# A hand-ordered software pipeline on every engine, exp(L) left in PSUM, and dummy matmuls first, in a fused gated-linear-attention and max-out kernel

## The chip, the cores and the metric

The kernel runs on one core of a Trainium2 chip. The metric is the device time of one execution in microseconds; lower is better. Here a run counts as slow when it is over 1.5% above the fastest run of the same kernel. A profile is one execution and covers its span, which is about 1.8 us shorter than the reported time. Below, "unit" is one step of the kernel's main loop: one chunk of 128 positions for two of the four batches. There are 12 units.

## The reference

```python
state = alpha[:, :, t, :, None] * state + einsum('bhd,bhe->bhde', k[:, :, t], v[:, :, t])   # for t in range(768)
y[:, :, t] = einsum('bhd,bhde->bhe', q[:, :, t], state)
x = y.transpose(0, 2, 1, 3).reshape(B * S, H * D)        # 3072 x 384
out = maximum(x @ w1, x @ w2) @ w_out                     # d_ff = 1024
```

B = 4, H = 8, S = 768, D = 48, all fp32. The kernel works in chunks: L is the running sum of log alpha in a chunk, q is scaled by exp(L), k by exp(-L), and the state is carried from chunk to chunk. The maximum is rewritten as relu(x(w1 - w2)) + x w2, so that x w2 w_out can be added by one small product, `w2o` = w2 w_out, made once.

## The kernel before

Each unit runs `gla(u)`: `lg` = Ln(alpha); the sums `cs` on TensorE; `Em` = exp(-L), `Ep` = exp(L) on ScalarE; `kn` = k x `Em` on GpSimd; `qn` = q x `Ep` on VectorE; transposes `tp`, copied to `qk`; the state products `kv`, added into `tm`; scores `pp`, masked into `pt`; outputs `ya`, cast to `xn`, transposed to `xp`, copied to `xt`. Then `moe(u-1)`: four hidden blocks `hp` with a relu into `gT`, and two output blocks `op`, copied to `outs`. A scheduler of the programming layer reorders what the program lists.

```python
nc.scalar.activation(out=Em, in_=csv[bb], func=ACTF.Exp, scale=-1.0)
nc.scalar.activation(out=Ep, in_=csv[bb], func=ACTF.Exp)                 # Ep in SBUF
nc.gpsimd.tensor_mul(out=kn[:, :, 0:D], in0=t["kf"][:, bb], in1=Em)
nc.vector.tensor_mul(out=qn[:, :, 0:D], in0=t["qf"][:, bb], in1=Ep)
# ... (cut)
for u in range(NU):
    if u + 3 < NU:
        load(u + 3)
    gla(u)
    if u == 0:
        weights()          # w2h -> transposes wt -> w2T; wo16; wq -> w2o; w12 = w1f - w2f
    if u - LAG >= 0:
        moe(u - LAG)       # LAG = 1
```

## Time and profile before

| | before |
|---|---|
| time, median (3 runs) | 189.61 us |
| span of the profile | 187.8 us |
| PE / DVE / ACT / POOL busy | 80 / 58 / 41 / 29% |
| period of a unit, undisturbed (125 to 139 us) | 13.15 us |
| first hidden matmul of unit 0 | 26.66 us |

The start: the timeline of the kernel before (start, duration, engine and line, instruction, and in brackets how long the engine idled before it and what ended that).

```profile
17.85 2.94 ACT L131 CAST w2h<-w2f 128x1024 f16<-128x1024 f32 x3
23.41 3.41 PE L142 MATMUL wq<-wo,w2T 128*128 128x384 f16 x20 [0.87 <-DVE wo L138]
27.39 1.36 PE L278 MATMUL hp<-xt,w 128*128 128x256 f16 x11 [0.46 <-ACT w2o L146]
30.29 0.50 PE L173 MATMUL cs<-lg,mc 64*128 64x384 f16 x4
```

The weights are cast and multiplied between 17.85 and 27 us, while the loads of unit 1 are still under way; its `cs` follows at 30.29.

### The profile page before, as it was taken

How to read it: one execution, taken by the hardware profiler on the slowest of the kernel's cores; microseconds unless marked ns; L12 is line 12 of the kernel's file. 1: busy time of each engine (PE TensorE's matmuls, PEld its weight loads, DVE VectorE, ACT ScalarE, POOL GpSimd, SP SyncE). 2: the span in 40 equal slices, each digit the busy share in tenths (PEclk: the TensorE clock that was granted, in tenths of full speed). 3: DMA queues.
4: the chain of work that ended last, by engine and by line, in shares of the span. 5: the costliest groups of instructions: out<-in, count | busy, mean ns of one | idle time of the engine just before them, and what ended most of it. 6: DMA issues, size and time to landing. Idle time of an engine off the chain costs nothing.

```text
span 187.8 us, 3984 instructions
## 1 busy us (share of the span) xinstructions
PE 149.7 (80%) x1632; PEld 98.8 (53%) x1632; DVE 109.4 (58%) x189; ACT 76.7 (41%) x163; POOL 53.7 (29%) x70
## 2 busy tenths in 40 slices
PE   0276799959997886976997896996996978969991
PEld 0063556627656545545554655654555545646660
DVE  4076773955939839647525846928919739358110
ACT  2503438237155361560236236346245364363331
POOL 5230302407208026035006407209018036061000
PEclk9999999966999999996579999999999999999999
DMA  4999999997998985969912994956957720020012
GB/s 106 188 338 377 378 187 186 169 246 152 194 182 206 201 210 105 162 162 153 155 31 87 199 168 130 204 103 165 172 141 152 133 84 5 0 84 3 10 74 84
DMA packets 92098, 28.56 MB, mean 152 GB/s; under 512 B 87216, under 2 KB 91312, under 8 KB 92080
## 3 DMA queue, kind: packets, MB, share of 16 engines
q1 hardware_dynamic: 88816, 23.60, 67.8%
q10 hardware_dynamic: 3264, 4.72, 6.8%
q8 instruction: 12, 0.20, 0.5%
q14 instruction: 6, 0.05, 0.1%
HBM read 23.59 MB, written 4.72 MB: 151 GB/s over the span
## 4 chain that ended last, share of the span: by engine, by line
PE 32%; issue 28%; DVE 17%; POOL 8%; ACT 7%; DMA 4%; ACTq 1%; SPq 1%; POOLq 0%; DVEq 0%
PE op L292 10%; DVE qn L190 6%; DVE pt L239 4%; PE op L290 4%; POOL kn L189 4%; DMA qf<-in_q_dram 4%; PE hp L278 3%; PE tp L194 3%; PE ya L256 3%; PE pp L237 2%; DVE tm L224 2%; DVE qk L196 2%; PE xp L265 2%; PE wq L142 2%; ACT outs L295 2%
## 5 line engine op out<-in xcount | busy, mean ns | idle before, releaser
L189 POOL TENSOR_TENSOR kn<-kf,Em 128x384 f16<-128x384 f32 x24 | 26.9, 1141 | 105.5 <-ACT Em L187 105.5
L190 DVE TENSOR_TENSOR qn<-qf,Ep 128x384 f16<-128x384 f32 x24 | 26.9, 1158 | 35.6 <-ACT Ep L188 28.9
L278 PE MATMUL hp<-xt,w 128*128 128x256 f16 x288 | 41.3, 284 | 2.0 <-ACT gT L283 1.5
L292 PE MATMUL op<-wo,gT 128*128 128x384 f16 x192 | 39.9, 333 | 0.3 <-DVE gT L285 0.3
L283 ACT ACTIVATE gT<-hp 128x512 f16<-128x512 f32 x36 | 20.8, 625 | 29.2 <-PE hp L278 29.1
L239 DVE TENSOR_TENSOR pt<-pp,u 128x512 f16<-128x512 f32 x48 | 31.2, 686 | 2.5 <-PE pp L237 1.9
L278 PEld LDWEIGHTS <-w 128*128 128x128 f16 x288 | 27.3, 101 | 7.1 <-issue 2.0
L260 ACT CAST xn<-ya 128x384 f16<-128x384 f32 x24 | 11.5, 477 | 31.1 <-PE ya L256 30.3
L295 ACT COPY outs<-op 128x384 f32<-128x384 f32 x24 | 11.5, 479 | 29.8 <-PE op L292 29.8
L292 PEld LDWEIGHTS <-gT 128*128 128x128 f16 x192 | 17.4, 99 | 10.3 <-DVE gT L285 1.5
L194 PE MATMUL tp<-ident,qn 128*128 128x128 f16 x96 | 9.9, 229 | 15.3 <-DVE qn L190 15.3
L290 PE MATMUL op<-w2o,xt 128*128 128x384 f16 x72 | 18.3, 332 | 0.2
L196 DVE COPY qk<-tp 128x1024 f16<-128x1024 f16 x24 | 16.2, 685 | 2.9 <-PE tp L194 2.0
L237 PE MATMUL pp<-qk 48*128 48x128 f16 x192 | 15.6, 232 | 1.3 <-DVE pt L239 0.9
L194 PEld LDWEIGHTS <-qn 128*128 128x128 f16 x96 | 6.1, 101 | 19.8 <-DVE qn L190 19.6
L267 DVE COPY xt<-xp 128x768 f16<-128x768 f16 x12 | 6.7, 557 | 16.1 <-PE xp L265 16.1
L256 PE MATMUL ya<-v,pt 128*128 128x48 f16 x192 | 13.5, 192 | 3.2 <-DVE pt L239 3.0
L187 ACT ACTIVATE Em<-cs 128x384 f32<-128x384 f32 x24 | 11.9, 494 | 8.1 <-PE cs L176 8.1
L256 PEld LDWEIGHTS <-pt 128*128 128x128 f16 x192 | 9.8, 101 | 9.7 <-DVE pt L239 4.7
L285 DVE TENSOR_SCALAR gT<-hp 128x512 f16<-128x512 f32 x12 | 8.2, 684 | 10.1 <-PE hp L278 10.0
L237 PEld LDWEIGHTS <-qk 48*128 48x128 f16 x192 | 9.4, 99 | 8.6 <-issue 5.0
L224 DVE TENSOR_TENSOR tm<-kv,sb 64x192 f32<-64x192 f32 x32 | 11.3, 354 | 1.5 <-PE kv L216 1.2
(48 smaller groups left out, 153.2 us busy)
## 6 DMA issues: line engine op xcount, KB each, us to landing
af<-in_alpha_dram SPq DMA_DIRECT2D x24, 192.0 KB, 5.0
kf<-in_k_dram SPq DMA_DIRECT2D x12, 384.0 KB, 5.0
qf<-in_q_dram SPq DMA_DIRECT2D x12, 384.0 KB, 7.0
vf<-in_v_dram SPq DMA_DIRECT2D x12, 384.0 KB, 7.5
out_dram<-outs ACTq DMA_DIRECT2D x12, 384.0 KB, 2.5
w2f<-in_moe_w_dram SPq DMA_DIRECT2D x1, 1536.0 KB, 8.5
wof<-in_moe_w_out_dram SPq DMA_DIRECT2D x1, 1536.0 KB, 10.6
w1f<-in_moe_w_dram SPq DMA_DIRECT2D x1, 1536.0 KB, 14.0
```

The lines of the kernel that those rows point to most:

```text
L189: nc.gpsimd.tensor_mul(out=kn[:, :, 0:D], in0=t["kf"][:, bb], in1=Em)
L190: nc.vector.tensor_mul(out=qn[:, :, 0:D], in0=t["qf"][:, bb], in1=Ep)
L194: nc.tensor.transpose(tp[:, n, j, :], pair(src, j), ident)
L196: nc.vector.tensor_copy(out=qk, in_=tp)
L237: nc.tensor.matmul(pa[a][:, j, :], lhsT=qk[r, 1, j, :], rhs=qk[r, 0, j, :], start=True, stop=True)
L239: nc.vector.tensor_mul(out=pt[:, a], in0=pa[a], in1=u16.unsqueeze(1).to_broadcast([128, HP, C]))
L256: nc.tensor.matmul(o, lhsT=l, rhs=r, start=a not in firsts, stop=(n >= len(mms) - 2))
L278: nc.tensor.matmul(hp[:, n, :], lhsT=w12[:, ds, f * 128 : (f + 1) * 128], rhs=xt[:, ds].rearrange("p n t -> p (n t)"), start=(ds == 0), st ...
L283: nc.scalar.activation(out=gT[:, 2 * f2 : 2 * f2 + 2, :], in_=hp, func=ACTF.Relu)
L290: nc.tensor.matmul(op, lhsT=xt[:, ds, n, :], rhs=w2o[:, ds, :], start=(ds == 0), stop=False)
L292: nc.tensor.matmul(op, lhsT=gT[:, f, n * C : (n + 1) * C], rhs=wo16[:, f, :], start=False, stop=(f == NF - 1))
L295: nc.scalar.copy(out=outs[:, n, :], in_=op)
```

## The change

The intent: TensorE should never wait for a chain of unit u, because between any two steps of that chain stands a piece of the MoE of unit u-1; every engine gets its program in a fixed order. exp(L) overwrites L in PSUM, so that `qn` no longer reads two SBUF operands (1158 ns in the mean in the kernel before). Twelve dummy matmuls on zeros come first, to warm TensorE's clock (the first `cs` group took 0.50 us with them and 0.82 without, E1). The steps are cut out of `gla` and `moe` as small functions (cut here). Smaller changes go with it: `kn` is transposed ahead of `qn`, `wo16` is cast on three engines and not on two, the loads are ordered earlier (unit u+5 at the end of iteration u, not u+3 at its start), and `outs` and `xt` have one buffer fewer each. The core is:

```diff
-            nc.scalar.activation(out=Ep, in_=csv[bb], func=ACTF.Exp)
+            nc.scalar.activation(out=csv[bb], in_=csv[bb], func=ACTF.Exp)
-            nc.vector.tensor_mul(out=qn[:, :, 0:D], in0=t["qf"][:, bb], in1=Ep)
+        nc.vector.tensor_mul(out=X["qn"][bb][:, :, 0:D], in0=X["qf"][:, bb], in1=X["csv"][bb])
+    ctx.enter_context(tc.manual_schedule())
+    warm = new("m", [128, 512], FP32, 2, "warm")
+    for n in range(NWARM):                                   # 12
+        nc.tensor.matmul(warm, lhsT=wz[:, 0:128], rhs=wz, start=True, stop=True)
+    load(1); ln(0); vcast(0); sums(0)                        # shortened to one line
+    for bb in range(2):
+        qmul(0, bb)
+        turn(0, bb)
+    ln(1)
+    vcast(1)
+    # loads of units 2 to 4 (cut)
+    for u in range(NU):
+        nxt = u + 1 < NU
+        kv(u)
+        pairs(u, 0)
+        fill(u, 0)
+        fill(u, 1)
+        if nxt:
+            sums(u + 1)
+        ystate(u)
+        pairs(u, 1)
+        fill(u, 2)
+        fill(u, 3)
+        if nxt:
+            state(u + 1)
+            for bb in range(2):
+                qmul(u + 1, bb)
+        yin(u)
+        fill(u, 4)
+        # turn(u + 1, 0), xturn(u), turn(u + 1, 1), fill(u, 5), ln(u + 2), vcast(u + 2), load(u + 5) (cut)
+    for n in range(6):
+        fill(NU, n)
```

`fill(u, 0..3)` are the hidden blocks and `fill(u, 4..5)` the output blocks of unit u-1; for u = 0 they are the preparation of the weights. `sums` also issues the exps and `kn`.

More of the change, by code (lines that the diff above doesn't have):

```diff
@@ L59 @@
     nc.scalar.preload_act_table_set("natural_log_exp_and_others")
-    loads = {}
+    st = {}
     def load(u):
         c, g = divmod(u, NG)
-        t = {}
+        t = st[u] = {}
         t["af"] = ldp.tile([128, H, 2, D], FP32, tag="af", name="af")
@@ L77, in load @@
             )
-        loads[u] = t
     load(0)
@@ L86 @@
     nc.sync.dma_start(out=w1f, in_=moe_w1.rearrange("(s p) f -> p s f", p=128))
+    NWARM = 12
+    wz = constp.tile([128, 512], FP16)
+    nc.vector.memset(wz, 0.0)
     mc = constp.tile([128, 2, C], FP16)
@@ L127 @@
     w2o = wp.tile([128, ND, DM], FP16)
-    def weights():
-        for ds in range(ND):
-            nc.scalar.copy(out=w2h[:, ds, :], in_=w2f[:, ds, :])
-            wt = psp.tile([128, NF, 128], FP16, tag="m", bufs=2, name="wt")
-            for f in range(NF):
-                nc.tensor.transpose(wt[:, f, :], w2h[:, ds, f * 128 : (f + 1) * 128], ident)
-            nc.vector.tensor_copy(out=w2T[:, :, ds * 128 : (ds + 1) * 128], in_=wt)
-        h2 = NF // 2
-        nc.gpsimd.tensor_copy(out=wo16[:, 0:h2], in_=wof[:, 0:h2])
-        nc.vector.tensor_copy(out=wo16[:, h2:NF], in_=wof[:, h2:NF])
-        for ds in range(ND):
-            wq = psp.tile([128, DM], FP32, tag="m", bufs=2, name="wq")
-            for f in range(NF):
-                nc.tensor.matmul(
-                    wq, lhsT=w2T[:, f, ds * 128 : (ds + 1) * 128], rhs=wo16[:, f, :],
-                    start=(f == 0), stop=(f == NF - 1),
-                )
-            nc.scalar.copy(out=w2o[:, ds, :], in_=wq)
-        for ds in range(ND):
-            nc.vector.tensor_sub(out=w12[:, ds, :], in0=w1f[:, ds, :], in1=w2f[:, ds, :])
@@ L150, with new @@
-    xts = {}
-    carry = {}
     def pair(t, j):
         return t[:, 2 * j : 2 * j + 2, :].rearrange("p h w -> p (h w)")
-    def gla(u):
-        c, g = divmod(u, NG)
-        t = loads.pop(u)
-        last = c == NCH - 1
-        lg = LG[u % NB]
-        nc.scalar.activation(
-            out=lg[:, :, :, 0:D], in_=t["af"].rearrange("p h j d -> p j h d"), func=ACTF.Ln
-        )
-        v16 = gp.tile([128, 2, H, D], FP16, tag="v16", name="v16")
-        nc.gpsimd.tensor_copy(out=v16, in_=t["vf"])
-        cs = [psp.tile([128, 512], FP32, tag="g", bufs=4, name="cs") for _ in range(2)]
-        csv = [x[:, 0 : H * D].rearrange("p (h d) -> p h d", h=H) for x in cs]
+    def new(tag, shape, dtype, bufs, name):
+        return psp.tile(shape, dtype, tag=tag, bufs=bufs, name=name)
@@ new lines, in ln, with vcast, sums @@
+    def ln(u):
+        X = st[u]
+        X["lg"] = LG[u % NB]
+        nc.scalar.activation(
+            out=X["lg"][:, :, :, 0:D], in_=X["af"].rearrange("p h j d -> p j h d"), func=ACTF.Ln
+        )
+    def vcast(u):
+        X = st[u]
+        X["v16"] = gp.tile([128, 2, H, D], FP16, tag="v16", name="v16")
+        nc.gpsimd.tensor_copy(out=X["v16"], in_=X["vf"])
+    def sums(u):
+        X = st[u]
+        c, g = divmod(u, NG)
+        lg = X["lg"]
+        cs = [new("g", [128, 512], FP32, 4, "cs") for _ in range(2)]
+        X["csv"] = csv = [x[:, 0 : H * D].rearrange("p (h d) -> p h d", h=H) for x in cs]
@@ L178, in gla @@
                 )
-        de = gp.tile([128, HP, 2, 2], FP32, tag="de", name="de")
-        qks = []
-        kns = []
+        X["qn"], X["kn"] = [], []
         for bb in range(2):
             qn, kn = QN[(2 * u + bb) % (2 * NB)], KN[(2 * u + bb) % (2 * NB)]
-            kns.append(kn)
-            Ep = gp.tile([128, H, D], FP32, tag="Ep", name="Ep")
+            X["qn"].append(qn)
+            X["kn"].append(kn)
             Em = gp.tile([128, H, D], FP32, tag="Em", name="Em")
             nc.scalar.activation(out=Em, in_=csv[bb], func=ACTF.Exp, scale=-1.0)
-            nc.scalar.activation(out=Ep, in_=csv[bb], func=ACTF.Exp)
-            nc.gpsimd.tensor_mul(out=kn[:, :, 0:D], in0=t["kf"][:, bb], in1=Em)
-            nc.vector.tensor_mul(out=qn[:, :, 0:D], in0=t["qf"][:, bb], in1=Ep)
-            tp = psp.tile([128, 2, HP, C], FP16, tag="g", bufs=4, name="tp")
-            for n, src in ((0, qn), (1, kn)):
-                for j in range(HP):
-                    nc.tensor.transpose(tp[:, n, j, :], pair(src, j), ident)
-            qk = gp.tile([128, 2, HP, C], FP16, tag="qk", name="qk")
-            nc.vector.tensor_copy(out=qk, in_=tp)
-            qks.append(qk)
+            nc.scalar.activation(out=csv[bb], in_=csv[bb], func=ACTF.Exp)
+            nc.gpsimd.tensor_mul(out=kn[:, :, 0:D], in0=X["kf"][:, bb], in1=Em)
@@ L198, in gla @@
+        X["de"] = de = gp.tile([128, HP, 2, 2], FP32, tag="de", name="de")
         nc.scalar.activation(out=de, in_=dps, func=ACTF.Exp)
-        sb = None
         if c:
-            tm, de0 = carry.pop(g)
+            Y = st[u - NG]
             dd = gp.tile([128, 2, HP], FP32, tag="dd", name="dd")
             nc.gpsimd.tensor_mul(
-                out=dd, in0=de0[:, :, :, 0].rearrange("p j b -> p b j"),
+                out=dd, in0=Y["de"][:, :, :, 0].rearrange("p j b -> p b j"),
                 in1=de[:, :, :, 1].rearrange("p j b -> p b j"),
@@ L208, in gla @@
             )
-            sb = gp.tile([128, 2, HP, D], FP16, tag="sb", name="sb")
-            nc.gpsimd.tensor_mul(out=sb, in0=tm, in1=dd.unsqueeze(3).to_broadcast([128, 2, HP, D]))
-        if not last:
-            tm = gp.tile([128, 2, HP, D], FP32, tag="tm", name="tm")
-            for bb in range(2):
-                kv = psp.tile([128, HP, 2 * D], FP32, tag="g", bufs=4, name="kv")
-                for j in range(HP):
-                    nc.tensor.matmul(
-                        kv[:, j, :], lhsT=pair(kns[bb], j), rhs=v16[:, bb, 2 * j : 2 * j + 2, :],
-                        start=True, stop=True,
-                    )
-                for a in range(2):
-                    r = slice(64 * a, 64 * a + 64)
-                    e = slice(D * a, D * a + D)
-                    if c:
-                        nc.vector.tensor_add(out=tm[r, bb], in0=kv[r, :, e], in1=sb[r, bb])
-                    else:
-                        nc.vector.tensor_copy(out=tm[r, bb], in_=kv[r, :, e])
-            carry[g] = (tm, de)
@@ L229, in gla, with state @@
-        pts = []
-        for bb in range(2):
-            qk = qks[bb]
-            pt = gp.tile([128, 2, HP, C], FP16, tag="pt", name="pt")
-            pa = [psp.tile([128, HP, C], FP32, tag="pp", bufs=2, name="pp") for _ in range(2)]
+            X["dd"] = dd
+    def state(u):
+        X = st[u]
+        if u >= NG:
+            X["sb"] = gp.tile([128, 2, HP, D], FP16, tag="sb", name="sb")
+            nc.gpsimd.tensor_mul(
+                out=X["sb"], in0=st[u - NG]["tm"], in1=X["dd"].unsqueeze(3).to_broadcast([128, 2, HP, D])
+            )
@@ new lines, in qmul, with turn @@
+    def qmul(u, bb):
+        X = st[u]
+        nc.vector.tensor_mul(out=X["qn"][bb][:, :, 0:D], in0=X["qf"][:, bb], in1=X["csv"][bb])
+    def turn(u, bb):
+        X = st[u]
+        tp = new("g", [128, 2, HP, C], FP16, 4, "tp")
+        for n, src in ((1, X["kn"][bb]), (0, X["qn"][bb])):
+            for j in range(HP):
+                nc.tensor.transpose(tp[:, n, j, :], pair(src, j), ident)
+        qk = gp.tile([128, 2, HP, C], FP16, tag="qk", name="qk")
+        nc.vector.tensor_copy(out=qk, in_=tp)
+        X["qk", bb] = qk
@@ new lines, in kv @@
+    def kv(u):
+        X = st[u]
+        c, g = divmod(u, NG)
+        if c == NCH - 1:
+            return
+        tm = X["tm"] = gp.tile([128, 2, HP, D], FP32, tag="tm", name="tm")
+        for bb in range(2):
+            kvp = new("g", [128, HP, 2 * D], FP32, 4, "kv")
+            for j in range(HP):
+                nc.tensor.matmul(
+                    kvp[:, j, :], lhsT=pair(X["kn"][bb], j), rhs=X["v16"][:, bb, 2 * j : 2 * j + 2, :],
+                    start=True, stop=True,
+                )
+            for a in range(2):
+                r = slice(64 * a, 64 * a + 64)
+                e = slice(D * a, D * a + D)
+                if c:
+                    nc.vector.tensor_add(out=tm[r, bb], in0=kvp[r, :, e], in1=X["sb"][r, bb])
+                else:
+                    nc.vector.tensor_copy(out=tm[r, bb], in_=kvp[r, :, e])
@@ new lines, in pairs @@
+    def pairs(u, bb):
+        X = st[u]
+        qk = X["qk", bb]
+        pt = X["pt", bb] = gp.tile([128, 2, HP, C], FP16, tag="pt", name="pt")
+        pa = [new("pp", [128, HP, C], FP32, 2, "pp") for _ in range(2)]
+        for j in range(HP):
+            for a in range(2):
+                r = slice(64 * a, 64 * a + D)
+                nc.tensor.matmul(pa[a][:, j, :], lhsT=qk[r, 1, j, :], rhs=qk[r, 0, j, :], start=True, stop=True)
+        for a in range(2):
+            nc.vector.tensor_mul(out=pt[:, a], in0=pa[a], in1=u16.unsqueeze(1).to_broadcast([128, HP, C]))
@@ L234, in gla, with ystate @@
+    def ystate(u):
+        X = st[u]
+        X["ya"] = ya = [new("g", [128, 2, HP, D], FP32, 4, "ya") for _ in range(2)]
+        X["begun"] = begun = set()
+        if u < NG:
+            return
+        for bb in range(2):
             for j in range(HP):
@@ L236, in gla @@
                     r = slice(64 * a, 64 * a + D)
-                    nc.tensor.matmul(pa[a][:, j, :], lhsT=qk[r, 1, j, :], rhs=qk[r, 0, j, :], start=True, stop=True)
-            for a in range(2):
-                nc.vector.tensor_mul(
-                    out=pt[:, a], in0=pa[a], in1=u16.unsqueeze(1).to_broadcast([128, HP, C])
-                )
-            pts.append(pt)
-        ya = [psp.tile([128, 2, HP, D], FP32, tag="g", bufs=4, name="ya") for _ in range(2)]
-        mms = [[], []]
-        for bb in range(2):
-            for j in range(HP):
-                for a in range(2):
-                    if c:
-                        r = slice(64 * a, 64 * a + D)
-                        mms[0].append((ya[a][:, bb, j, :], qks[bb][r, 0, j, :], sb[r, bb, j, :], a))
-                    mms[1].append((ya[a][:, bb, j, :], pts[bb][:, a, j, :], v16[:, bb, 2 * j + a, :], a))
@@ L253, in gla @@
-        mms = mms[0] + mms[1]
-        firsts = set()
-        for n, (o, l, r, a) in enumerate(mms):
-            nc.tensor.matmul(o, lhsT=l, rhs=r, start=a not in firsts, stop=(n >= len(mms) - 2))
-            firsts.add(a)
-        xn = gp.tile([128, 2, HP, 2, D], FP16, tag="xn", name="xn")
+                    nc.tensor.matmul(
+                        ya[a][:, bb, j, :], lhsT=X["qk", bb][r, 0, j, :], rhs=X["sb"][r, bb, j, :],
+                        start=a not in begun, stop=False,
+                    )
@@ new lines, in ystate, with yin @@
+                    begun.add(a)
+    def yin(u):
+        X = st[u]
+        ya, begun = X["ya"], X["begun"]
+        for bb in range(2):
+            for a in range(2):
+                for j in range(HP):
+                    nc.tensor.matmul(
+                        ya[a][:, bb, j, :], lhsT=X["pt", bb][:, a, j, :], rhs=X["v16"][:, bb, 2 * j + a, :],
+                        start=a not in begun, stop=(bb == 1 and j == HP - 1),
+                    )
+                    begun.add(a)
+        X["xn"] = xn = gp.tile([128, 2, HP, 2, D], FP16, tag="xn", name="xn")
@@ L259, in gla, with xturn @@
         for a in range(2):
             nc.scalar.copy(out=xn[:, :, :, a, :], in_=ya[a])
-        xp = psp.tile([128, ND, 2, C], FP16, tag="g", bufs=4, name="xp")
+    def xturn(u):
+        X = st[u]
+        xp = new("g", [128, ND, 2, C], FP16, 4, "xp")
         for bb in range(2):
-            xf = xn[:, bb].rearrange("p j a d -> p (j a d)")
+            xf = X["xn"][:, bb].rearrange("p j a d -> p (j a d)")
             for ds in range(ND):
                 nc.tensor.transpose(xp[:, ds, bb, :], xf[:, ds * 128 : (ds + 1) * 128], ident)
-        xts[u] = mp.tile([128, ND, 2, C], FP16, tag="xt", bufs=4, name="xt")
@@ L267, in gla @@
-        nc.vector.tensor_copy(out=xts[u], in_=xp)
-    def moe(u):
-        c, g = divmod(u, NG)
-        xt = xts.pop(u)
-        gT = mp.tile([128, NF, 2 * C], FP16, tag="gT", name="gT")
-        for f2 in range(NF // 2):
-            hp = psp.tile([128, 2, 2 * C], FP32, tag="m", bufs=2, name="hp")
-            for n in range(2):
-                f = 2 * f2 + n
-                for ds in range(ND):
-                    nc.tensor.matmul(
-                        hp[:, n, :], lhsT=w12[:, ds, f * 128 : (f + 1) * 128],
-                        rhs=xt[:, ds].rearrange("p n t -> p (n t)"), start=(ds == 0), stop=(ds == ND - 1),
-                    )
-            if f2 % 4 != 3:
-                nc.scalar.activation(out=gT[:, 2 * f2 : 2 * f2 + 2, :], in_=hp, func=ACTF.Relu)
-            else:
-                nc.vector.tensor_relu(out=gT[:, 2 * f2 : 2 * f2 + 2, :], in_=hp)
-        outs = mp.tile([128, 2, DM], FP32, tag="outs", bufs=3, name="outs")
-        for n in range(2):
-            op = psp.tile([128, DM], FP32, tag="m", bufs=2, name="op")
-            for ds in range(ND):
-                nc.tensor.matmul(op, lhsT=xt[:, ds, n, :], rhs=w2o[:, ds, :], start=(ds == 0), stop=False)
-            for f in range(NF):
-                nc.tensor.matmul(
-                    op, lhsT=gT[:, f, n * C : (n + 1) * C], rhs=wo16[:, f, :], start=False, stop=(f == NF - 1)
-                )
-            nc.scalar.copy(out=outs[:, n, :], in_=op)
-        nc.scalar.dma_start(
-            out=out.rearrange("(b s) d -> s b d", b=B)[c * C : (c + 1) * C, 2 * g : 2 * g + 2, :], in_=outs
-        )
@@ L300, with hid @@
-    LAG = 1
-    for u in range(1, 3):
+        X["xt"] = mp.tile([128, ND, 2, C], FP16, tag="xt", bufs=3, name="xt")
+        nc.vector.tensor_copy(out=X["xt"], in_=xp)
+    def hid(u, f2):
+        X = st[u]
+        if f2 == 0:
+            X["gT"] = mp.tile([128, NF, 2 * C], FP16, tag="gT", name="gT")
+        gT = X["gT"]
+        hp = new("m", [128, 2, 2 * C], FP32, 2, "hp")
+        for n in range(2):
+            f = 2 * f2 + n
+            for ds in range(ND):
+                nc.tensor.matmul(
+                    hp[:, n, :], lhsT=w12[:, ds, f * 128 : (f + 1) * 128],
+                    rhs=X["xt"][:, ds].rearrange("p n t -> p (n t)"), start=(ds == 0), stop=(ds == ND - 1),
+                )
+        if f2 < 3:
+            nc.scalar.activation(out=gT[:, 2 * f2 : 2 * f2 + 2, :], in_=hp, func=ACTF.Relu)
+        else:
+            nc.vector.tensor_relu(out=gT[:, 2 * f2 : 2 * f2 + 2, :], in_=hp)
@@ new lines, in outp @@
+    def outp(u, n):
+        X = st[u]
+        c, g = divmod(u, NG)
+        if n == 0:
+            X["outs"] = mp.tile([128, 2, DM], FP32, tag="outs", bufs=2, name="outs")
+        op = new("m", [128, DM], FP32, 2, "op")
+        for ds in range(ND):
+            nc.tensor.matmul(op, lhsT=X["xt"][:, ds, n, :], rhs=w2o[:, ds, :], start=(ds == 0), stop=False)
+        for f in range(NF):
+            nc.tensor.matmul(
+                op, lhsT=X["gT"][:, f, n * C : (n + 1) * C], rhs=wo16[:, f, :], start=False, stop=(f == NF - 1)
+            )
+        nc.scalar.copy(out=X["outs"][:, n, :], in_=op)
+        if n == 1:
+            nc.scalar.dma_start(
+                out=out.rearrange("(b s) d -> s b d", b=B)[c * C : (c + 1) * C, 2 * g : 2 * g + 2, :], in_=X["outs"]
+            )
@@ new lines, in wturn, with wmul @@
+    def wturn(ds):
+        nc.scalar.copy(out=w2h[:, ds, :], in_=w2f[:, ds, :])
+        wt = new("m", [128, NF, 128], FP16, 2, "wt")
+        for f in range(NF):
+            nc.tensor.transpose(wt[:, f, :], w2h[:, ds, f * 128 : (f + 1) * 128], ident)
+        nc.vector.tensor_copy(out=w2T[:, :, ds * 128 : (ds + 1) * 128], in_=wt)
+    def wmul(ds):
+        wq = new("m", [128, DM], FP32, 2, "wq")
+        for f in range(NF):
+            nc.tensor.matmul(
+                wq, lhsT=w2T[:, f, ds * 128 : (ds + 1) * 128], rhs=wo16[:, f, :],
+                start=(f == 0), stop=(f == NF - 1),
+            )
+        nc.scalar.copy(out=w2o[:, ds, :], in_=wq)
@@ new lines, in fill @@
+    def fill(u, n):
+        if u > 0:
+            hid(u - 1, n) if n < 4 else outp(u - 1, n - 4)
+        elif n < 3:
+            wturn(n)
+        elif n == 3:
+            nc.gpsimd.tensor_copy(out=wo16[:, 0:2], in_=wof[:, 0:2])
+            nc.vector.tensor_copy(out=wo16[:, 2:5], in_=wof[:, 2:5])
+            nc.scalar.copy(out=wo16[:, 5:NF], in_=wof[:, 5:NF])
+        elif n == 4:
+            wmul(0)
+            wmul(1)
+        else:
+            wmul(2)
+            for ds in range(ND):
+                nc.vector.tensor_sub(out=w12[:, ds, :], in0=w1f[:, ds, :], in1=w2f[:, ds, :])
@@ L302 @@
+    ctx.enter_context(tc.manual_schedule())
+    warm = new("m", [128, 512], FP32, 2, "warm")
+    for n in range(NWARM):
+        nc.tensor.matmul(warm, lhsT=wz[:, 0:128], rhs=wz, start=True, stop=True)
+    load(1)
+    ln(0)
+    vcast(0)
+    sums(0)
+    for bb in range(2):
+        qmul(0, bb)
+        turn(0, bb)
+    ln(1)
+    vcast(1)
+    for u in range(2, 5):
         load(u)
     for u in range(NU):
-        if u + 3 < NU:
-            load(u + 3)
-        gla(u)
-        if u == 0:
-            weights()
@@ L309 @@
-        if u - LAG >= 0:
-            moe(u - LAG)
-    for u in range(NU - LAG, NU):
-        moe(u)
+        nxt = u + 1 < NU
[11 more added lines that the diff above has]
+            state(u + 1)
+            for bb in range(2):
+                qmul(u + 1, bb)
+        yin(u)
+        fill(u, 4)
+        if nxt:
+            turn(u + 1, 0)
@@ L316 @@
+        xturn(u)
+        if nxt:
+            turn(u + 1, 1)
+        fill(u, 5)
+        if u + 2 < NU:
+            ln(u + 2)
+            vcast(u + 2)
+        if u + 5 < NU:
+            load(u + 5)
+    for n in range(6):
+        fill(NU, n)
 _INS = ['q', 'k', 'v', 'alpha', 'moe_w1', 'moe_w2', 'moe_w_out']
```

## The prediction

> **What bounds the kernel now.** I read the page first: busy shares and the slices.
>
> ```profile
> PE 149.7 (80%) x1632; PEld 98.8 (53%) x1632; DVE 109.4 (58%) x189; ACT 76.7 (41%) x163; POOL 53.7 (29%) x70
> ...
> PE   0276799959997886976997896996996978969991
> ...
> PEclk9999999966999999996579999999999999999999
> DMA  4999999997998985969912994956957720020012
> ```
>
> No engine is full. Loads keep the DMA engines at nine tenths only up to about slice 9 and in patches to slice 31. TensorE is the fullest, never at nine for long, and the granted clock falls twice. Next I read the timeline of one undisturbed unit in the second half (start, duration, engine, instructions, and in brackets the idle time before and its releaser).
>
> ```profile
> 125.56 0.48 ACT L295 COPY outs<-op 128x384 f32<-128x384 f32 x1 [1.31 <-PE op L292]
> 126.10 1.47 PE L278 MATMUL hp<-xt,w 128*128 128x256 f16 x12
> 127.12 2.27 POOL L189 TENSOR_TENSOR kn<-kf,Em 128x384 f16<-128x384 f32 x2 [8.72 <-ACT Em L187]
> 127.45 2.35 DVE L190 TENSOR_TENSOR qn<-qf,Ep 128x384 f16<-128x384 f32 x2 [3.29 <-ACT Ep L188]
> 128.59 0.40 PE L194 MATMUL tp<-ident,qn 128*128 128x128 f16 x4 [1.01 <-DVE qn L190]
> 129.86 0.40 PE L194 MATMUL tp<-ident,qn 128*128 128x128 f16 x4 [0.54 <-DVE qn L190]
> 133.35 0.38 PE L237 MATMUL pp<-qk 48*128 48x128 f16 x4 [0.43 <-DVE pt L239]
> 138.72 0.48 ACT L295 COPY outs<-op 128x384 f32<-128x384 f32 x1 [1.73 <-PE op L292]
> ```
>
> The period is 138.72 - 125.56 = 13.16 us. The sums `cs` of the next unit are only issued when the previous MoE's output is through, so exp, `qn`/`kn`, transposes, `pt`, `ya`, `xn`, `xp` follow as one long chain, with too little MoE work left to cover it: PE idles 1.01 + 0.54 + 0.43 us, and later runs `pp`/`ya` in scraps of four. The chain of waits agrees (DVE `qn`, DVE `tm`, DVE `pt`, PE, ACT `xn` in turn). The costliest suspicious group:
>
> ```profile
> L189 POOL TENSOR_TENSOR kn<-kf,Em 128x384 f16<-128x384 f32 x24 | 26.9, 1141 | 105.5 <-ACT Em L187 105.5
> L190 DVE TENSOR_TENSOR qn<-qf,Ep 128x384 f16<-128x384 f32 x24 | 26.9, 1158 | 35.6 <-ACT Ep L188 28.9
> ```
>
> By instruction, `qn` lasts from 545 to 1355 ns and `kn` from 993 to 1322, for one shape: they run at the same time and hinder each other.
>
> Last, the start. In the timeline the first hidden-layer matmul of unit 0 comes at 27.39 us, since weights (`w2h`, 17.85) and unit 0 are prepared while unit 1 is loading; the last hidden-layer block of unit 11 ends at 179.9. From 27.39 to 176.63, the start of the last MoE, are 11 units of 13.57 us, which include the slow-clock stretches.
>
> [...] a 128x384 matmul comes every 0.16 us late in the run, and the clock records are 0.5 from 38.6 to 45.4 and 86.4 to 96.6 us, each just after a patchy stretch. It was also slow before 21.5 us (eight `wt` transposes took 0.93), though the records show no event there. [...] the chain has eight in 1.31 us, 164 ns. [...] four transposes 0.23 us apart from the next four, 57 ns each. [...]
>
> **The change part by part.**
>
> *exp in place in PSUM.* `qn` then reads one PSUM and one SBUF operand. I take its undisturbed 0.55 us, and 1.0 for `kn`. VectorE saves 24 x 0.6 = 14 us of busy time, GpSimd 3 us. The exp itself costs ScalarE the same 0.5. VectorE per unit becomes: 2 `qn` 1.1, 2 `qk` 1.4, 4 `tm` 1.45, 4 `pt` 2.7, `xt` 0.56, one relu 0.69: 7.9 us. ScalarE stays at 6.8 (`lg` 0.85, five exps 1.75, `xn` 1.07, three relus 1.75, `outs` 0.96, output issue 0.38), GpSimd at 4.2 (`kn` 2.0, `v16` 0.82, `dd` 0.5, `sb` 0.83).
>
> *The order.* What TensorE needs for a unit, from start-to-start times where it ran undisturbed: `cs` 0.44, `halves` 0.21, 24 `hp` at 0.108 = 2.6, 22 `op` at 0.163 = 3.6, 16 `tp` 0.9, 8 `kv` 0.35, 16 `pp` 0.6, 16 state `ya` 0.55, 16 `ya` 0.55, 6 `xp` 0.35: 10.15 us. I walked the new order through one iteration by hand with these durations, starting at `kv`. `tm` frees the first banks at 2.0; `pt` of half 0 ends at 3.35 where PE could want its banks at 3.15; `pt` of half 1 ends at 5.2 while PE does two hidden blocks, `yin` waits some 0.2 for its last four; `qn` of the next unit ends near 7, `xn` near 7.0, both before PE leaves the first output block at 7.6; `qk`, `xt`, `qk` are copied under the second output block. Relus come in time for the two `m` banks. So stalls add about 0.4 to 0.6: period 10.7 us, PE-bound. At that density the clock should not fall back.
>
> *The start gets worse.* ScalarE's program now has `ln(1)` ahead of `w2h`, and TensorE has `cs` of unit 1 ahead of the second half of unit 0. Unit 1's `af` is loaded behind 4.7 MB of weights: its completion record stands at 26.7 us (issued at 10.94), `vf` of unit 1 at 33.4, and GpSimd's cast of that `vf` now stands ahead of `kn(1)` and of its part of `wo16`. Then, with the old durations: `lg` 27.6, two `w2h` 29.5, `cs` about 31, exps 33.2, third `w2h` 34.2, ScalarE's part of `wo16` 35.4, GpSimd's 37.0; `wq` 37 to about 41 (16 matmuls partly at half rate), `tp`/`xp`/`tp` 42, last `wq` 43.5. VectorE copies to 43.2, and only then subtracts for `w12`, 3.5 us: 46.7. So unit 0's first hidden block starts near 46.7 against 27.39: 19 us later. Iteration 1 starts at 43.5, is held by `w12` and the pile of `tm` and `pt` behind it, and ends near 56.2.
>
> *Dummies.* [...] They cost nothing, and what they warm is idle from about 15 to 28 us: worth about 0.
>
> *Sum.* 56.2, then iterations 2 to 10, 9 x 10.7 = 96.3; iteration 11 lacks the next unit's `cs`, `tp` and its `kv`, 10.7 - 1.9 = 8.8; iteration 10 lacks `kv`, -0.35; last MoE 6.2 + 0.2; tail from the last matmul 4.1 as now (183.7 to 187.8). Span 171.5; reported times stand 1.8 above the span: 173.3 us, 0.914 of 189.6.
>
> **The rivals.** *The fixed order adds waits of its own.* Each engine now stalls on its first unready instruction, where before a scheduler picked. VectorE has 10.7 - 7.9 = 2.8 us of slack per unit, ScalarE 3.9; for it speaks that `pt` twice comes out within 0.2 us of need. The sum above is 66.3 + 10 periods, so at 12.3 us the whole gain is gone, 189. I think up to 11.5 likely enough, 181. *Loads become the bound.* A unit is 1.57 MB in and 0.39 MB out; in 30 to 50 us the windows show 177 to 206 GB/s: about 10.3 us per unit, close to 10.7. Against: four sets of buffers and a late start give the queue a lead of about two units, and until the first output it needs only 8.3. If it bites, about 176. *The start is shorter*, since TensorE may warm sooner or `w12`'s parts overlap more: 168. *Only scheduling noise, the same time*: that would need iteration 1 to end at 72 us instead of 56.
>
> **Range and chances.** Every 0.1 us of period is 1 us of time. Periods from 10.2 (no stalls) to 11.5 give 168 to 181; the start adds +-3. Range 166 to 182. Slower needs a period over 12.6, so 0.03; within 2% 0.06; faster 0.91.
>
> **What would show it.** First `hp` at 45 to 48 us, with `w2h` waiting behind `lg`, which waits for `af`; repeated `outs` 10.4 to 11 us apart from unit 2 on, clock at nine in all those slices, PE in nines; `qn` mean about 0.55 and `kn` 1.0; PE's waits under 0.7 us a unit; loads landing a unit or more ahead of use. I am wrong if the first `hp` comes before 40, if PE waits over 1.5 us a unit for `pt`, `qn` or gT, if `qn` stays near 1.1, or if `lg` waits for `af` after unit 3.

## The result, and the profile after

The changed kernel took 168.69 us at the median (167.21 to 171.49, four runs), the kernel before 189.88 in the same rounds. The ratio is 0.888 (95% interval 0.878 to 0.897). Ratios here are the mean time of one kernel's fast runs over that of the other's of the same rounds, so not quite the ratio of the medians quoted. The prediction was 173, range 166 to 182.

The profile that came with this result was slow (span 169.8 us), so the lines are from a later, fast execution of the same kernel (E0 below, span 165.3). First its page (the slices are counted from 0):

```profile
PE 136.7 (83%) x1644; PEld 97.1 (59%) x1644; DVE 95.0 (57%) x190; ACT 77.7 (47%) x164; POOL 46.7 (28%) x70
...
PE   6706103489389999999999999999999999999990
...
PEclk9965555559999999999999999999999999999997
DMA  3999999999999969889699796998999702020202
```

From slice 12 on TensorE is at nine in every slice, and its clock stays full; before, that row was patchy to the end. The price is on the left: in slices 4 to 7 TensorE is busy for four tenths at most, and in slices 3 to 8 the granted clock stands at half. The busy time of VectorE fell from 109.4 to 95.0 us. Now one unit in the timeline:

```profile
107.73 0.50 PE L160 MATMUL cs<-lg,mc 64*128 64x384 f16 x4
109.18 1.96 POOL L175 TENSOR_TENSOR kn<-kf,Em 128x384 f16<-128x384 f32 x2 [5.65 <-PE pp L239]
111.28 1.01 DVE L198 TENSOR_TENSOR qn<-qf,cs 128x384 f16<-128x384 f32 x2
112.69 0.39 PE L205 MATMUL tp<-ident,kn 128*128 128x128 f16 x4
117.89 0.50 PE L160 MATMUL cs<-lg,mc 64*128 64x384 f16 x4
```

The period is 117.89 - 107.73 = 10.16 us (10.15 in the others), against 13.15. No PE line has an idle bracket. `kn` and `qn` are now done one after the other, and the transposes start 0.4 us after the second `qn`. The windows view sums it up, busy time by engine in a stretch (start:end, length, then PE, PEld, DVE, ACT, POOL with the instructions of each, then clock, DMA share and GB/s). First the kernel before, then the changed one:

```profile
100.00:165.00 65.00, 55.51 (x670) 36.32 (x668) 42.02 (x66) 29.42 (x65) 22.54 (x26) 1.00 0.66 126
```

```profile
55.00:154.00 99.00, 98.78 (x1315) 72.94 (x1313) 68.72 (x128) 56.33 (x124) 32.95 (x44) 1.00 0.83 156
```

TensorE was occupied for 85% of the one stretch and 99.8% of the other. (The profile models the ends of matmuls, so both are rather too high; E5 tests the reading.) These are the start lines of the changed kernel:

```profile
25.55 0.84 ACT L141 ACTIVATE lg<-af 128x768 f16<-128x768 f32 x1 [16.57 <-DMA af<-in_alpha_dram]
26.30 1.98 ACT L321 CAST w2h<-w2f 128x1024 f16<-128x1024 f32 x2
35.43 3.50 PE L330 MATMUL wq<-wo,w2T 128*128 128x384 f16 x16 [0.55 <-POOL wo L343]
41.09 4.11 DVE L352 TENSOR_TENSOR w<-w1f,w2f 128x1024 f16<-128x1024 f32 x3
42.35 0.28 PE L293 MATMUL hp<-xt,w 128*128 128x256 f16 x1 [0.23 <-DVE w L352]
```

ScalarE idles 16.57 us for alpha of unit 1 with the weight casts behind it, although the weights they need landed at 15.2. So `wq` starts 13.7 us later than before (35.43 against 21.72) and the first hidden block 15.7 us later.

All of it fits one sum. I cut each span at the first `hp` and at the last unit's first `hp`:

| | to the first hidden block | eleven units | last MoE and tail | span |
|---|---|---|---|---|
| before | 26.66 | 149.97 (13.63 each) | 11.15 | 187.8 |
| after (E0) | 42.35 | 111.73 (10.16 each) | 11.18 | 165.3 |

38.2 us are gained in the stretch of the eleven units and 15.7 lost at the start: 22.5 net. Some of the 38.2 is the half-rate stretches of the kernel before: 13.63 - 13.15 = 0.48 a unit, 5.3 us. And the two profiles are not alike: the one before is slow (granted clock 0.955), E0 is the fastest of its six runs. The fast runs beside E0 differ by 19.2 us (means 187.2 and 168.0), so about 3 of the 22.5 us lie in which executions were profiled. The periods of 13.15 and 10.15 are not touched by this, as the clock was full in both stretches.

### The profile page after: what moved, and what is told of

Its sections match the earlier page's. It is cut to its first block, busy times and chain, and to the rows that moved or that the text cites. A ratio compares the mean times of both kernels' runs of the same rounds, so it can differ in the third digit from the quotient of the medians.

```text
span 169.8 us, 4029 instructions
## 1 busy us (share of the span) xinstructions
PE 140.2 (83%) x1644; PEld 98.7 (58%) x1644; DVE 94.5 (56%) x190; ACT 77.8 (46%) x164; POOL 46.2 (27%) x70
## 4 chain that ended last, share of the span: by engine, by line
PE 71%; issue 17%; POOL 5%; DVE 3%; ACT 2%; ACTq 0%; POOLq 0%
PE hp L293 19%; PE op L311 19%; PE op L309 7%; PE tp L205 6%; PE pp L239 4%; PE wq L330 3%; PE cs L160 3%; PE ya L265 3%; POOL kn L175 2%; PE xp L280 2%; DVE w L352 2%; PE ya L253 2%; PE cs L163 2%; PE kv L219 2%; POOL v L148 1%
## 5 line engine op out<-in xcount | busy, mean ns | idle before, releaser
L175 POOL TENSOR_TENSOR kn<-kf,Em 128x384 f16<-128x384 f32 x24 | 23.5, 998 | 60.4 <-ACT Em L172 33.2
L293 PE MATMUL hp<-xt,w 128*128 128x256 f16 x288 | 37.4, 280 | 2.2 <-DVE w L352 1.9
L311 PE MATMUL op<-wo,gT 128*128 128x384 f16 x192 | 35.3, 327 | 0.0
L207 DVE COPY qk<-tp 128x1024 f16<-128x1024 f16 x24 | 16.5, 687 | 20.7 <-PE tp L205 20.7
L141 ACT ACTIVATE lg<-af 128x768 f16<-128x768 f32 x12 | 10.1, 843 | 25.6 <-DMA af<-in_alpha_dram 20.9
L148 POOL CAST v<-vf 128x768 f16<-128x768 f32 x12 | 9.9, 823 | 38.9 <-DMA vf<-in_v_dram 38.9
L198 DVE TENSOR_TENSOR qn<-qf,cs 128x384 f16<-128x384 f32 x24 | 12.2, 546 | 6.1 <-DMA qf<-in_q_dram 6.1
L205 PE MATMUL tp<-ident,kn 128*128 128x128 f16 x96 | 9.7, 226 | 6.2 <-POOL kn L175 6.2
L205 PEld LDWEIGHTS <-kn 128*128 128x128 f16 x96 | 7.0, 101 | 8.1 <-POOL kn L175 6.5
L174 ACT ACTIVATE cs<-cs 128x384 f32<-128x384 f32 x24 | 11.8, 490 | 0.0
L239 PE MATMUL pp<-qk 48*128 48x128 f16 x192 | 11.7, 228 | 0.0
## 6 DMA issues: line engine op xcount, KB each, us to landing
wof<-in_moe_w_out_dram SPq DMA_DIRECT2D x1, 1536.0 KB, 10.7
```

Of the source, the lines that this page charges most:

```text
L174: nc.scalar.activation(out=csv[bb], in_=csv[bb], func=ACTF.Exp)
L175: nc.gpsimd.tensor_mul(out=kn[:, :, 0:D], in0=X["kf"][:, bb], in1=Em)
L198: nc.vector.tensor_mul(out=X["qn"][bb][:, :, 0:D], in0=X["qf"][:, bb], in1=X["csv"][bb])
L205: nc.tensor.transpose(tp[:, n, j, :], pair(src, j), ident)
L207: nc.vector.tensor_copy(out=qk, in_=tp)
L239: nc.tensor.matmul(pa[a][:, j, :], lhsT=qk[r, 1, j, :], rhs=qk[r, 0, j, :], start=True, stop=True)
```

## The experiments

All results are right unless it is said otherwise. E0 to E2 and E7 ran on one chip with shared runs of the kernel before (median 188.4), E3 to E6 on a second (189.5), E8 to E10 on a third (188.8), E11 on a fourth (189.5). For E3, E4, E6 and E8 to E11 the record's own verdict is "unclear"; only three runs of the kernel before were fast on each of those chips.

**E0, the changed kernel again.** No edit.

> The changed kernel once more, beside the kernels it is compared with. Both theories: 167 to 169 us, ratio 0.88 to 0.90. In its profile the period of the sums should be 10.15 us again from unit 3 on.

168.41 us (167.06 to 171.43), ratio 0.898 (0.890 to 0.905). This is the reference for what follows.

**E1, without the dummies.**

```diff
-    warm = new("m", [128, 512], FP32, 2, "warm")
-    for n in range(NWARM):
-        nc.tensor.matmul(warm, lhsT=wz[:, 0:128], rhs=wz, start=True, stop=True)
```

> The twelve dummy matmuls left out, nothing else. My theory: they only speed up cs of unit 0 (0.8 us instead of 0.44), and the start is set by the loads (af of unit 1 complete at 26.3 us), so the time stays within 0.7 us of the changed kernel. Rival: the dummies are a working part of the gain (a warm clock for unit 0), then 2 us or more slower.

168.05 us, ratio 0.899 (0.891 to 0.906). The dummies are worth nothing here. They do what they are meant to: with them the first `cs` group is 0.50 us long instead of 0.82. After the next idle, of 6.0 us, the first four transposes took 0.61 us with and without them (0.39 late in the run). But nothing that sets the time waits for it.

**E2, exp(L) to SBUF again, in the fixed order.**

```diff
-            nc.scalar.activation(out=csv[bb], in_=csv[bb], func=ACTF.Exp)
+            Ep = gp.tile([128, H, D], FP32, tag="Ep", name="Ep")
+            nc.scalar.activation(out=Ep, in_=csv[bb], func=ACTF.Exp)
-        nc.vector.tensor_mul(..., in0=X["qf"][:, bb], in1=X["csv"][bb])
+        nc.vector.tensor_mul(..., in0=X["qf"][:, bb], in1=X["Ep", bb])
```

> The changed kernel with exp(L) written to SBUF again, order kept. My theory: in the new order kn ends before qn starts, so qn meets only dd and sb on GpSimd, costs at most 0.8 us more per unit, and that lies in the 0.7 us or so by which qn precedes its transposes: time within 1 us of the changed kernel, period 10.15 to 10.3. Rival: the in-place exp is what makes the order work; qn back at 1.1 us, period 10.8 or more, 8 us slower.

168.08 us, ratio 0.897 (0.890 to 0.903), period 10.13 us. The group in the profile of E2, and of E0 below it (count, busy time, mean ns, idle before):

```profile
L200 DVE TENSOR_TENSOR qn<-qf,Ep 128x384 f16<-128x384 f32 x24 | 18.1, 791 | 6.1 <-DMA qf<-in_q_dram 6.1
```

```profile
L198 DVE TENSOR_TENSOR qn<-qf,cs 128x384 f16<-128x384 f32 x24 | 12.2, 546 | 6.2 <-DMA qf<-in_q_dram 6.2
```

`qn` does get slower, 791 ns instead of 546. It is not back at the 1158 of the kernel before, since `kn` is over by then and only `sb` and the tail of the small `dd` run beside it. The 0.5 us a unit disappear in slack: VectorE is not what the period waits for.

**E3, the kernel before with exp(L) in place.**

```diff
-            Ep = gp.tile([128, H, D], FP32, tag="Ep", name="Ep")
-            nc.scalar.activation(out=Ep, in_=csv[bb], func=ACTF.Exp)
+            nc.scalar.activation(out=csv[bb], in_=csv[bb], func=ACTF.Exp)
-            nc.vector.tensor_mul(out=qn[:, :, 0:D], in0=t["qf"][:, bb], in1=Ep)
+            nc.vector.tensor_mul(out=qn[:, :, 0:D], in0=t["qf"][:, bb], in1=csv[bb])
```

> The kernel before with only exp(L) in place in PSUM, scheduler on. My theory: there the two qn (0.8 and 1.36 us, slowed by kn) stand on the chain of each unit; at 0.55 each the period falls by about 1 us: 177 to 183 us, ratio 0.93 to 0.97. Rival: the in-place exp gives little by itself since the fixed order is the whole gain: ratio 0.98 to 1.0.

180.09 us, ratio 0.959 (0.949 to 0.970); late periods 12.23 us instead of 13.15. So the same edit is worth 4% in the old order and nothing in the new one. In the old order `qn` stood on the chain that a unit waited for, and its overlap with `kn` lengthened it (means of 1158 ns for `qn` and 1141 for `kn` in the kernel before, 553 and 1000 in E3); the new order takes it off that chain. TensorE's two waits for `qn` in a unit, 1.01 and 0.54 us in the kernel before, are one in E3:

```profile
122.71 0.40 PE L193 MATMUL tp<-ident,qn 128*128 128x128 f16 x4 [0.49 <-DVE qn L189]
```

The two gains overlap and must not be added.

**E4, the changed program with the scheduler on.**

```diff
-    ctx.enter_context(tc.manual_schedule())
```

> The changed program with the scheduler left on: same pieces and buffers, no fixed order. My theory: the fixed order gives the period of 10.15 us but costs some 15 us at the start; with the scheduler the first hidden block comes before 38 us and the period is longer, 11 to 12.5: 166 to 180 us. Rival: the pieces themselves are the gain and the scheduler keeps the period at 10.2, then 155 to 162 us.

172.88 us, ratio 0.922 (0.913 to 0.931): inside the range of my theory. The first hidden block comes at 34.33 us, the period is 11.77. Two lines of one unit of E4:

```profile
114.00 0.38 PE L205 MATMUL tp<-ident,kn 128*128 128x128 f16 x4 [0.32 <-ACT xn L272]
116.39 0.40 PE L239 MATMUL pp<-qk 48*128 48x128 f16 x8 [0.34 <-DVE qk L207]
```

The scheduler leaves two waits per unit, 0.66 us together, and splits `pp` and `op` in parts. Its period of 11.77 must be held against E3's 12.23, not against 13.15, since E4 has exp(L) in place too: the new program with its pieces and buffers gives the scheduler 0.46 us a unit, and the fixed order takes another 1.62 (to 10.15) and gives back some of it at the start. Of the 1.62 the two waits explain 0.66; the rest is not accounted for here.

**E5, without the x times w2o matmuls** (relative error 1.0). Its output is wrong, which doesn't matter for the time.

```diff
-        for ds in range(ND):
-            nc.tensor.matmul(op, lhsT=X["xt"][:, ds, n, :], rhs=w2o[:, ds, :], start=(ds == 0), stop=False)
         for f in range(NF):
-            nc.tensor.matmul(op, ..., start=False, stop=(f == NF - 1))
+            nc.tensor.matmul(op, ..., start=(f == 0), stop=(f == NF - 1))
```

> The six matmuls of a unit that add x times w2o are left out: the result is wrong on purpose. My theory: the period is TensorE's own work, so it falls by 6 x 0.164 = 0.98 us to 9.2 and the time by 10 to 12 us, to 156 to 158. Rival: a chain over VectorE or ScalarE is as long as TensorE's work; then less than 5 us.

158.48 us at the median; the two fast runs are 157.61 and 156.75, about 11 below E0's fast runs (mean 168.0). The period fell from 10.15 to 9.18, by 0.97, which is the work taken away, 6 x 0.164. TensorE's own work is the period, and at 9.18 no other engine was the bound yet. The start of one unit's sums and of the next one's:

```profile
104.20 0.50 PE L160 MATMUL cs<-lg,mc 64*128 64x384 f16 x4
113.38 0.50 PE L160 MATMUL cs<-lg,mc 64*128 64x384 f16 x4
```

**E10, the fixed order without the interleave.**

```diff
-        fill(u, 0)
-        fill(u, 1)
-        fill(u, 2)          # each at its place
-        fill(u, 3)
-        fill(u, 4)
-        fill(u, 5)
+        for n in range(6):  # behind the steps of unit u
+            fill(u, n)
```

> The fixed order without the interleave: all six MoE pieces of an iteration stand behind the steps of its unit. My theory: the steps then wait for VectorE, ScalarE and GpSimd with nothing to fill; by hand the steps last 7.5 to 8 us and the pieces 6.2: period 13.5 to 14.5 us, 200 to 215 us, slower than the kernel before. Rival: what pays is the other changes (exp in place, buffers, kn first), then below 185 us.

216.98 us, ratio 1.164 (1.152 to 1.175), slightly beyond the range: the sums come 14.3 to 15.5 us apart. Two lines of one unit:

```profile
105.34 0.50 PE L160 MATMUL cs<-lg,mc 64*128 64x384 f16 x4 [1.25 <-ACT lg L141]
107.68 0.34 PE L265 MATMUL ya<-v,pt 128*128 128x48 f16 x4 [0.44 <-DVE pt L241]
```

The waits I expected are there. What I had not counted is the clock: it fell to half rate once in every iteration, eleven times from 49 us on, for 47.8 us together (mean granted clock 0.818, against 0.911 in E0). In these stretches four transposes took 0.43 us from start to start, and 0.22 outside them. If that work had run at the full rate it would have taken half of this, so the clock is at most 24 of the 49 us (an estimate). Another 9 are the start, for the weights are prepared behind unit 0's steps too and the first hidden block comes at 51.63 us. A fixed order by itself is no gain; a bad one is worse than the scheduler's.

**E7, dummies where TensorE idles.** 42 dummy matmuls between the first `pp` of unit 0 and the weight transposes.

```diff
         nc.scalar.copy(out=w2h[:, ds, :], in_=w2f[:, ds, :])
+        if ds == 0:
+            wm = new("m", [128, 512], FP32, 2, "wm")
+            for n in range(42):
+                nc.tensor.matmul(wm, lhsT=wz[:, 0:128], rhs=wz, start=True, stop=True)
```

> 42 further dummy matmuls on TensorE between the first pp of unit 0 and the weight transposes, where TensorE idles from 17 to 28 us. My theory: the start is partly bound by a half-rate clock (16 wq matmuls took 5.24 us instead of 2.6): 2.5 to 5 us faster than the changed kernel. Rival: the start is bound by the copies on VectorE, ScalarE and GpSimd and by w12, so within 1 us.

170.45 us (169.98 to 170.74), ratio 0.910 (0.904 to 0.916): 2 us slower, so both theories missed. In its profile the clock is full from 20.7 to 34.3 us, which is when TensorE has little useful work, and at half rate from 34.3 to 41.2, when `wq` runs: 4.45 us for 16 against 3.50 in E0. Also v of unit 1 came later, and with it GpSimd's `wo16`, for which `wq` waits (GpSimd first, then TensorE):

```profile
33.64 0.82 POOL L148 CAST v<-vf 128x768 f16<-128x768 f32 x1 [19.39 <-DMA vf<-in_v_dram]
```

```profile
37.70 4.45 PE L334 MATMUL wq<-wo,w2T 128*128 128x384 f16 x16 [3.43 <-POOL wo L347]
```

In E0 the two stand at 31.88 and 35.43, so 2.3 us were lost before `wq` and another 0.95 in it. The dummies shifted the slow stretch rather than removing it. Whether they also delayed the load stays open: in the profiles of E0, E1, E2, E5, E9 and the slow one, which have no such dummies, this cast began between 31.88 and 33.27 us, not far below 33.64.

**E9, the smallest mending of the start.**

```diff
-    ln(1)
-    vcast(1)
 ...
         fill(u, 1)
+        if u == 0:
+            ln(1)
         if nxt:
             sums(u + 1)
+        if u == 0:
+            vcast(1)
```

> The smallest mending of the start: only ln(1) is moved behind the first two w2h on ScalarE and the cast of v of unit 1 behind kn on GpSimd; TensorE's order is untouched. My theory: cs of unit 1 on TensorE still holds the second half of unit 0, the weights product and w12 until alpha of unit 1 has come; wq starts near 33.5 instead of 35.4: 165.5 to 167.5 us. Rival: ScalarE's wait alone was the loss, then 158 to 161 us, as with the whole start reordered.

168.24 us, ratio 0.903 (0.891 to 0.916): nothing gained, against both. The casts `w2h` ran at 15.19 us as intended, but TensorE then idled 7.5 us for `cs` of unit 1, `wq` still waited for GpSimd's part of `wo16`, which I had left behind the cast of v, and began at 34.91 instead of 35.43; and it took 5.09 us at half rate. One wait removed let the next one end the start. TensorE's two waits in E9:

```profile
26.59 0.82 PE L160 MATMUL cs<-lg,mc 64*128 64x384 f16 x4 [7.50 <-ACT lg L141]
34.91 5.09 PE L330 MATMUL wq<-wo,w2T 128*128 128x384 f16 x16 [2.73 <-POOL wo L343]
```

**E6, the whole start reordered.** All of unit 0 and the weights go ahead of unit 1 on every engine; from iteration 1 the order is unchanged but for the two hidden blocks done early. The casts of v of units 0 to 2 stand behind the `sums` of their units, that is behind `kn`.

```diff
+    kv(0); pairs(0, 0); pairs(0, 1); wturn(0); ystate(0); yin(0)     # one step a line in the kernel
+    wturn(1); xturn(0); wturn(2); fill(0, 3); fill(0, 4); fill(0, 5)
+    load(5)
+    ln(1); sums(1); vcast(1); qmul(1, 0); qmul(1, 1)
+    hid(0, 0); hid(0, 1); turn(1, 0); turn(1, 1); ln(2)
-    for u in range(NU):
+    for u in range(1, NU):
         # fill(u, 0), fill(u, 1) only for u > 1; vcast(2) behind sums(2)
```

> All of unit 0 and of the weights is put ahead of unit 1 on every engine, two hidden blocks of unit 0 ahead of unit 1's transposes, and the cast of v behind kn; from iteration 1 on the order is unchanged. My theory: the start costs the changed kernel what its order makes wait for af of unit 1; the first hidden block comes at 28 to 31 us instead of 45, iteration 2 starts 5 to 9 us earlier, then the loads of units 2 and 3 hold it: 159 to 164 us. Rival: loads bind anyway, less than 3 us gained.

159.40 us, ratio 0.848 (0.835 to 0.860): it beats both kernels. From its timeline:

```profile
16.67 1.04 PE L324 MATMUL wt<-ident,w2h 128*128 128x128 f16 x8
29.75 1.47 PE L293 MATMUL hp<-xt,w 128*128 128x256 f16 x12
36.83 0.82 PE L160 MATMUL cs<-lg,mc 64*128 64x384 f16 x4 [1.71 <-ACT lg L141]
```

The first hidden block is 12.6 us earlier than in E0. Only about 9 of these reach the end: TensorE then waits for alpha of unit 2, as the third line shows, and the clock falls (36.8 to 40.2).

**E8, the waits of E6 filled.** The other two hidden blocks of unit 0 go before `kv` of unit 1, and unit 0's output blocks take the hidden blocks' places in iteration 1.

```diff
+    fill(0, 4); ln(1); fill(0, 5); load(5)
+    hid(0, 0); sums(1); vcast(1); qmul(1, 0); qmul(1, 1)
+    hid(0, 1); turn(1, 0); turn(1, 1); hid(0, 2); hid(0, 3); ln(2)
     # iteration 1: outp(0, 0) for fill 0 and 1, outp(0, 1) for fill 2 and 3, none for 4 and 5
```

> As the reordered start, but the other two hidden blocks of unit 0 are put where TensorE still waited (before kv of unit 1) and its two output blocks take the places of the hidden blocks in iteration 1; ln of unit 1 before the last w2o. My theory: in the reordered start TensorE still idles some 4 us between 28 and 37 us for v and alpha of units 1 and 2; filled with unit 0's MoE, iteration 2 starts 2.5 to 4 us earlier: 155 to 157 us. Rival: the loads of unit 3 then hold iteration 2 and the time stays at 158 to 160.

159.43 us, ratio 0.856 (0.847 to 0.864): the rival was right. Iteration 2 did start earlier, at 43.22 us instead of 45.81, and lost it again (GpSimd first, then TensorE):

```profile
51.48 0.82 POOL L148 CAST v<-vf 128x768 f16<-128x768 f32 x1 [8.11 <-DMA vf<-in_v_dram]
```

```profile
53.31 0.40 PE L205 MATMUL tp<-ident,kn 128*128 128x128 f16 x4 [2.44 <-POOL kn L175]
```

`kn` of unit 3, whose k had landed, stood on GpSimd behind the cast of a v that had not.

**E11, kn ahead of the cast in every unit.**

```diff
             for bb in range(2):
                 qmul(u + 1, bb)
+            vcast(u + 1)     # E8's `if u == 1: vcast(2)` goes (cut)
 ...
         if u + 2 < NU:
             ln(u + 2)
-            vcast(u + 2)
```

> The filled start with GpSimd's cast of v of every unit moved behind kn and the state of that unit. My theory: the filled start gained nothing since iteration 2 stopped at 50.7 us for kn of unit 3, which stood behind the cast of a v that landed at 51.4 us, and the clock fell in the gap (2.4 us of waiting, then 3.4 us at half rate); with kn first, TensorE reaches iteration 3 at 53 to 54 us instead of 58: 154 to 157 us. Rival: the loads themselves (k and q of units 3 and 4) are as late as v, and it stays at 158 to 160 us.

157.23 us (156.13 to 158.97), ratio 0.838 (0.828 to 0.848), the best of all. Iteration 3 starts at 54.96 us instead of 57.98, and the clock does not fall again after 28.5 us. Both are just outside what was expected: 54.96 against 53 to 54 us, 157.23 against 154 to 157. The intervals of E6, E8 and E11 overlap or nearly touch and they ran on different chips, so E11's lead over E6 is likely, not certain; all three are clearly faster than the changed kernel.

## Why the prediction was right

The measured 168.7 lies in the range, 4.6 us under the sum's 173.3; the span of E0 lies 6.2 us under the 171.5 of the sum (the mean of E0's fast spans, 166.3, lies 5.2 under). The mechanism was right: a period set by TensorE's work, and a start made worse by waits for unit 1's loads. It was not luck with opposite errors, as nearly all of the difference lies on one side. By its own terms:

- *The period, 10.7 us.* The TensorE sum of 10.15 was right to the second digit; the step that was off is "stalls add about 0.4 to 0.6", which measured 0.0. Iterations 2 to 10 took 146.17 - 54.78 = 91.4 us instead of 95.95: 4.6 of the 6.2 us. I had carried each hand-walked coincidence of 0.1 to 0.3 us (`pt` against `pp`, `pt` against `yin`) into the period. PE's row has no gap there; with 99.8% occupied such a stall did not show. E5 shows that the period is TensorE's work alone.
- *Iteration 11* took 7.9 us instead of 8.8, for the same reason; the last MoE 7.1 instead of 6.4. These nearly cancel. The 6.4 was a misreading: in the trace of the kernel before the same stretch already took 7.1 (176.63 to 183.7).
- *The start gets worse.* Right in mechanism and nearly in size: iteration 1 ended at 54.8, predicted 56.2; the first `hp` came at 42.35 (45.14 in the slow profile), predicted 46.7. (The 27.39 that it took for the kernel before is the second group; the first `hp` stands at 26.66, so 19 was really 20 us by its figures, and 15.7 was measured.) The loads of unit 1 were used 1.2 to 1.5 us earlier than in the profile I took them from. That an engine holds the work behind its wait was the prediction's assumption; E0 shows it for ScalarE, 16.57 us. The prediction named three waits: ScalarE's `lg`, TensorE's `cs` and GpSimd's v. ScalarE's alone was not the cause: E9 moved it, and v behind `kn`, and gained nothing. That the three together made the start is shown by E6, which undoes all; TensorE's `cs` alone was not tested.
- *exp in place.* The durations were right (546 ns and 1.00 us; VectorE saved 14.4 us, predicted 14). Measured over the runs, `qn` with two SBUF inputs took 1158 ns in the mean beside `kn` and 791 beside `sb` (E2), but 546 with one input in PSUM, though `sb` ran beside it there too, and 553 beside `kn` (E3). I gave it no term on the path, and E2 shows that this was right in the new order. I did not say that in the old order it is worth 7.6 us (E3, means of the fast runs: 180.0 against 187.6).
- *Dummies worth 0.* Right (E1).
- *The rivals.* No waits of the fixed order's own once the loop ran, no bound by loads: DMA stayed busy at six to nine tenths into slice 31 and TensorE did not feel it. The rival of a shorter start named 168, close to what was measured, but by another route: the start gave 1.4 us and the period 4.6. Loads did become what the next step meets, in E6 and E8. "At that density the clock should not fall back" holds in E0's profile (granted clock 1.00 from 55 to 154 us); in the slow one it fell once more, from 48.4 to 55.2 us, just behind the `w12` waits. E0's profile is the exception rather: the fast profiles of E2, E5, E7 and E9 show such a fall too, of 3.4 to 6.8 us between 44.8 and 51.6, and the other fast runs of E0 have a granted clock of 0.895 to 0.896 against its 0.911.
- *The signs.* Two of those named did not come: the `outs` were 10.15 us apart and not 10.4 to 11, and the first `hp` fell into 45 to 48 us only in the slow profile. None of the signs of being wrong came: `lg` waited for `af` only for units 0 and 1.

## What to carry to other kernels

When TensorE waits on a chain of other engines, lay other work between the links rather than shorten the links: here the same steps without the interleave took 217 us instead of 168 (9 of the 49 at the start, up to 24 by the clock), and with it a 0.25 us faster `qn` was worth nothing. A fixed order is strict at the start too: put nothing whose data comes late ahead of work whose data is there (ScalarE idled 16.57 us in E0 for alpha, with the weight casts behind it), and check every engine, for moving one wait only shows the next (E9 against E6; E8 against E11). And work out TensorE's own time per iteration from start-to-start times; if the order leaves no waits, that is the period (here 10.15 us).

## What the profiles showed of TensorE's clock and of the transposes

- In E10 the granted clock fell to half eleven times from 49 us on, once an iteration, where the longest gap seen between matmuls was 1.59 us. What in those stretches made it fall was not tested.
- The transposes here, each with its weight load, came in fours 0.22 to 0.23 us apart at the full clock, 56 ns each.
- Dummies ahead of a wait did not pay here: with 42 of them this kernel was 2 us slower (E7), and the half-rate stretch stood at 34.3 to 41.2 us. By which path the time was lost is not settled.
